# ACT's first weight load waits for GpSimd's identity matrix

## The chip, the cores and the metric

The kernel runs on one core of a Trainium2 chip. A core has five engines with queues of their own: TensorE (PE, matrix multiplies; PEld is its weight loads), VectorE (DVE), ScalarE (ACT), GpSimd (POOL) and SyncE (SP, which here only issues DMAs). They work at the same time and wait for each other by semaphores. DMAs are issued from SP and from ACT, each into a queue of its own, and are moved by 16 DMA engines that both queues share. The metric is the device time in microseconds of one execution; before the change it is 168.63 us, the median of 3 runs (168.02 to 168.94).

## The reference

Two branches work on the same input `x` (2048 positions of 512 values, bfloat16) and are mixed by a gate that each position computes for itself:

```python
x = A_x
g = _sigmoid((x * gate_w).sum(-1, keepdims=True))
a = _A_ref(x, A_wqkv, A_wo)
b = _B_ref(x, B_w1, B_b1, B_w2, B_b2)
return g * a + (1 - g) * b
```

Branch A is local attention: `x @ wqkv` gives queries, keys and values for 32 heads of 16 values. Each position attends to 8 positions, itself and those 2, 4, ... 14 before it; the result is multiplied by `wo`. Branch B is a layer norm over the 512 values of a position, followed by a two-layer network with a gelu that mixes over the 2048 positions (`w1` is 2048 x 1792, `w2` is 1792 x 2048).

## The kernel before, in words

Everything is kept in one SBUF arena and cut into tiles of 128 partitions. TensorE's work comes in four stages: the projections to queries, keys and values (line 619), the sums over a head's 16 values for the attention scores (line 698), the two layers of branch B (lines 812 and 862), and the output projection (line 878). VectorE does the attention's products and sums and the final mixing, ScalarE takes results out of PSUM and applies exp and gelu.

The kernel is first written down as a list of operations, each with its engine, its estimated duration, what it reads and writes and what it must wait for (`deps`: a wait on a semaphore; `order`: only a place in the order). A planner (`schedule`) then simulates the engines with these estimates and fixes the order on each engine; `plan_waits` leaves out the waits that are already implied. For the first loads the planner's landing times are given by hand (`lands`), and their `deps` are cleared, so that they are issued as early as their queue comes to them.

The projections need `x` transposed: 512 positions of a block along the free axis and the 512 values along partitions. Block 0 (the first 512 positions) is built from two sources:

- The first 128 values of each position are loaded as they stand, as "plain columns" (`d_xp`, line 479, SP's first DMA: 512 runs of 256 bytes, 128 KB). TensorE transposes them by multiplying with an identity matrix (`tr0`, `tr1`, line 545). ScalarE copies one half of the result out of PSUM (`ev_tra`, line 555) and VectorE the other (`ev_trb`, line 557).
- The other 384 values are transposed by the DMA itself (`d_xt0`, line 473, SP's second DMA).

The identity matrix is made by GpSimd (`ident`, line 417), its first operation after the constants. `tr0` waits for it, and VectorE's `rp` (line 424), which sums its columns into a small indicator matrix.

The query weights come in four loads of 128 rows each (`d_wp0_0` to `d_wp0_3`, 128 KB each, all with line 429). The first two are ACT's first two instructions, followed by the load of ACT's function table and `ev_tra`. The last two are issued by SP after `d_xt0`, and after them the key weights, `x` itself for the layer norm (`d_x0` and on), and the transposed reads of the later blocks (`d_xt1` and on, line 460).

TensorE begins with seven warm-up matmuls on constants (line 537), goes on with the four transposing matmuls, one more warm-up matmul, and then block 0's projections (`pf_...`, line 619): four that need `d_wp0_0` and the transposed plain columns, four that need `d_wp0_1` and `d_xt0`, four for `d_wp0_2`, four for `d_wp0_3`, then the keys' sixteen.

Of the kernel before, what the change touches and what calls it, by code (L numbers as in the profile page):

```python
# [333 lines left out]
def bass_gated_mix__sliding_local_dilated__mixer_token_mlp__prompt_kernel(nc, A_x, A_wqkv, A_wo, B_x, B_w1, B_b1, B_w2, B_b2, gate_w, out, dbg=None):  # L334
    with contextlib.ExitStack() as es:
# [75 lines left out]
        def psub(ap_, p0, np_, offs, dims):  # L411
# [5 lines left out]
        c_ident = A("pool", lambda e: e.affine_select(out=IDENT, in_=nc.const_aps.tensor(1.0, [128, 128], BF16), pattern=[[1, 128]], compare_op=ALU.is_equal,  # L417
                                                     fill=0.0, base=0, channel_multiplier=-1),
                    0.4, writes=["ident"], name="ident")
# [19 lines left out]
        def ld_x(t0, n, q="sp"):  # L439
            ds = sch.dsem("x%d" % t0)  # L440
            op = sch.dma(q, mk_dma(X[:, t0:t0 + n, :], xv[:, t0:t0 + n, :]), n * 128 * D * 2, ds,
                         writes=["x%d" % t for t in range(t0, t0 + n)], deps=throttle() if q == "sp" else [], after=prev_dma() if q == "sp" else [], name="d_x%d" % t0)
            if q == "sp":
                init_dmas.append(op)
            return op

        def ld_w(tn, d0, n, q="sp"):
            ds = sch.dsem("wqkv%d_%d" % (tn, d0))
            op = sch.dma(q, mk_dma(WQKV[:, d0:d0 + n, tn * D:(tn + 1) * D], wqkv_v[:, d0:d0 + n, tn * D:(tn + 1) * D]),
                         n * 128 * D * 2, ds, writes=["wqkv%d_%d" % (tn, dt) for dt in range(d0, d0 + n)],  # L450
                         deps=throttle() if q == "sp" and n == 4 else [], after=prev_dma() if q == "sp" else [],
                         issue=0.65 if n == 4 else 0.45, name="d_wp%d_%d" % (tn, d0))
            if q == "sp":
                init_dmas.append(op)
            return op
# [14 lines left out]
        def ld_xt0():  # L470
            ds = sch.dsem("xt0")
            dst = XT[:, 1:4, 0:512]
            op = sch.dma("sp", lambda e: e.dma_start_transpose(dst, x2d[0:512, 128:512]), 512 * 384 * 2, ds, issue=1.25,
                         writes=XT0[1:4], after=prev_dma(), name="d_xt0")
            init_dmas.append(op)
            return op
# [6 lines left out]
        first_loads = [ld_w(0, 0, 1, "act"), ld_xt0(), ld_w(0, 1, 1, "act"), ld_w(0, 2, 1), ld_w(0, 3, 1), ld_w(1, 0, 2), ld_w(1, 2, 2),  # L483
                       ld_x(0, 2)]
        ld_xt(1)
        first_loads.append(init_dmas[-1])
        for op_, t_ in zip(first_loads, (3.5, 5.7, 5.0, 6.3, 6.7, 7.6, 8.6, 9.4, 11.0)):
            op_.lands = t_
            op_.deps.clear()
        first_loads[2].order.add(first_loads[0])  # L490
        init_dmas[:] = [first_loads[1]] + first_loads[5:]
        ld_x(2, 2)
# [560 lines left out]
```

## Time and profile before

| | |
|---|---|
| median of 3 runs | 168.63 us (168.02 to 168.94) |
| the profiled execution | 168.55 us |
| its span, first to last instruction | 167.3 us |
| TensorE matmuls busy | 163.9 us (98%) |
| VectorE busy | 151.3 us (90%) |
| ScalarE busy | 75.0 us (45%) |
| GpSimd busy | 0.7 us |
| DMA | 29.64 MB, mean 177 GB/s |

The span is what the profile shows of one execution, from its first to its last instruction; some time lies around it. Busy time of TensorE is an upper bound, since matmuls are pipelined and overlap. The profile names groups of instructions by the line of the kernel, so that all plain DMAs, which one helper issues, have line 429, and are told apart by their tensors, engines and times. Times in the timeline are counted from the start of the span.

### The profile page before, as it was taken

How to read it: one execution, taken by the hardware profiler on the slowest of the kernel's cores; microseconds unless marked ns; L12 is line 12 of the kernel's file. 1: busy time of each engine (PE TensorE's matmuls, PEld its weight loads, DVE VectorE, ACT ScalarE, POOL GpSimd, SP SyncE). 2: the span in 40 equal slices, each digit the busy share in tenths (PEclk: the TensorE clock that was granted, in tenths of full speed). 3: DMA queues.
4: the chain of work that ended last, by engine and by line, in shares of the span. 5: the costliest groups of instructions: out<-in, count | busy, mean ns of one | idle time of the engine just before them, and what ended most of it. 6: DMA issues, size and time to landing. Idle time of an engine off the chain costs nothing.

```text
span 167.3 us, 2152 instructions
## 1 busy us (share of the span) xinstructions
PE 163.9 (98%) x860; PEld 77.6 (46%) x860; DVE 151.3 (90%) x154; ACT 75.0 (45%) x116; POOL 0.7 (0%) x8
## 2 busy tenths in 40 slices
PE   7999999999999999999999999999999999999994
PEld 2455555554454444444444444444444444444463
DVE  0145999999999999999999999999999999999896
ACT  3077688889899818793113121131231321310100
POOL 1000000000000000000000000000000000000000
DMA  5999999968003837996579936462672580000454
GB/s 130 315 272 262 303 322 291 307 196 246 0 0 97 311 115 187 303 290 153 133 183 343 335 129 143 112 187 68 184 218 83 138 223 0 0 0 0 157 190 159
DMA packets 47625, 29.64 MB, mean 177 GB/s; under 512 B 9856, under 2 KB 46464, under 8 KB 47616
## 3 DMA queue, kind: packets, MB, share of 16 engines
q1 hardware_dynamic: 45504, 24.85, 54.0%
q10 hardware_dynamic: 2112, 4.66, 10.0%
q8 instruction: 7, 0.11, 0.3%
q14 instruction: 2, 0.02, 0.0%
HBM read 21.24 MB, written 2.10 MB: 140 GB/s over the span
## 4 chain that ended last, share of the span: by engine, by line
PE 94%; DVE 3%; DMA 2%; issue 0%
PE ps L812 29%; PE ps L862 29%; PE ps L619 25%; PE ps L878 6%; PE ps L698 4%; DVE arena L899 2%; DMA arena<-in_A_x_dram 2%; PE ps L545 0%; DVE arena L557 0%
## 5 line engine op out<-in xcount | busy, mean ns | idle before, releaser
L812 PE MATMUL ps<-arena 128*128 128x512 bf16 x224 | 48.7, 379 | 0.0
L862 PE MATMUL ps<-arena 128*128 128x512 bf16 x224 | 48.7, 379 | 0.0
L619 PE MATMUL ps<-arena 128*128 128x512 bf16 x192 | 42.3, 382 | 0.1
L690 DVE TENSOR_TENSOR arena<-arena 128x4096 bf16<-128x4096 bf16 (+1 forms) x12 | 35.5, 2996 | 2.3 <-ACT arena L630 1.8
L797 DVE TENSOR_TENSOR arena<-arena 128x8192 bf16<-128x8192 bf16 x8 | 35.0, 4419 | 0.0
L812 PEld LDWEIGHTS ps<-arena 128*128 128x128 bf16 x224 | 21.8, 98 | 26.7 <-ACT arena L728 0.4
L862 PEld LDWEIGHTS ps<-arena 128*128 128x128 bf16 x224 | 21.9, 98 | 26.5
L619 PEld LDWEIGHTS ps<-arena 128*128 128x128 bf16 x192 | 21.6, 114 | 20.8 <-DVE arena L557 0.7
L930 ACT ACTIVATE arena<-ps,arena 128x512 bf16<-128x512 f32 x16 | 12.4, 778 | 39.4 <-PE ps L862 39.4
L800 DVE TENSOR_TENSOR arena<-arena 128x4096 bf16<-128x4096 bf16 (+1 forms) x16 | 27.0, 1752 | 0.0
L630 ACT ACTIVATE arena<-ps 128x512 bf16<-128x512 f32 x32 | 18.5, 596 | 4.5 <-PE ps L619 4.5
L833 ACT ACTIVATE arena<-ps,arena 128x512 bf16<-128x512 f32 x14 | 9.6, 687 | 22.2 <-PE ps L812 17.4
L574 DVE BATCH_NORM_STATS2 arena<-arena 128x6 f32<-128x512 bf16 x16 | 10.0, 680 | 5.6 <-DMA arena<-in_A_x_dram 5.6
L878 PE MATMUL ps<-arena 128*128 128x512 bf16 (+1 forms) x80 | 14.2, 337 | 0.0
L899 DVE SCALAR_TENSOR_TENSOR arena<-ps,arena 128x512 bf16<-128x512 f32 (+1 forms) x20 | 11.5, 638 | 0.9 <-PE ps L878 0.7
L598 ACT ACTIVATE arena<-arena 128x512 bf16<-128x512 bf16 x16 | 12.2, 806 | 0.0
L627 ACT ACTIVATE arena<-ps 128x512 bf16<-128x512 f32 x16 | 9.0, 596 | 5.5 <-PE ps L619 5.4
L878 PEld LDWEIGHTS ps<-arena 128*128 128x128 bf16 x80 | 7.8, 98 | 6.3
L674 DVE SCALAR_TENSOR_TENSOR arena<-arena 128x512 bf16<-128x512 bf16 x16 | 10.1, 685 | 0.0
L744 DVE TENSOR_TENSOR arena<-arena 128x512 bf16<-128x512 bf16 (+4 forms) x11 | 7.3, 667 | 0.6 <-ACT arena L763 0.2
L698 PE MATMUL ps<-arena 128*32 128x512 bf16 x128 | 7.3, 380 | 0.0
L728 ACT ACTIVATE arena<-ps 128x512 bf16<-128x512 f32 x8 | 4.7, 592 | 4.6 <-PE ps L698 4.6
(42 smaller groups left out, 40.5 us busy)
## 6 DMA issues: line engine op xcount, KB each, us to landing
arena<-in_B_w_dram SPq DMA_DIRECT2D x7, 1024.0 KB, 8.3
arena<-in_B_w_dram SPq DMA_DIRECT2D x8, 896.0 KB, 5.1
arena<-arena ACTq DMA_DIRECT2D x32, 128.0 KB, 3.0
arena<-in_A_x_dram SPq DMA_DIRECT2D x4, 512.0 KB, 5.1
out_dram<-arena SPq DMA_DIRECT2D x14, 128.0 KB, 1.7
arena<-in_A_x_dram SPq DMA_DIRECT2D x1, 1536.0 KB, 7.9
arena<-in_A_wqkv_dram SPq DMA_DIRECT2D x2, 256.0 KB, 3.6
arena<-in_A_x_dram SPq DMA_DIRECT2D x2, 256.0 KB, 3.5
```

The source lines that it names most:

```text
L598: A("act", (lambda t_: (lambda e: e.activation(out=X[:, t_, :], in_=X[:, t_, :], func=AF.Identity, scale=col(RSTD, t_), bias=col(NMR, t_)) ...
L619: ins = e.matmul(ps[:, bank, s0:s1], lhsT=lhsT, rhs=XT[:, dt, sb * 512 + s0:sb * 512 + s1], start=(dt == 0 and s0 == 0), stop=(dt == 3))
L630: return lambda e: e.activation(out=dst, in_=ps[:, bank, :], func=AF.Copy)
L690: return lambda e: e.tensor_tensor(out=PBL[buf][:, :, 512 * c0:512 * (c0 + nc_)], in0=in0, in1=in1, op=ALU.mult)
L698: ins = e.matmul(ps[32 * c:32 * c + 32, 4 + wl, :], lhsT=RP, rhs=PBL[buf][:, wl, c * 512:(c + 1) * 512], start=(dl == 0), stop=(dl == 3), ...
L797: A("dve", (lambda o_, i0, i1: (lambda e: e.tensor_tensor(out=o_, in0=i0, in1=i1, op=ALU.mult)))(pv, in0, in1), 4.4, reads=v_res + ["atx_% ...
L800: A("dve", (lambda pv_, n__: (lambda e: e.tensor_tensor(out=pv_[:, 0:n__], in0=pv_[:, 0:n__], in1=pv_[:, n__:2 * n__], op=ALU.add)))(pv, n ...
L812: ins = e.matmul(ps[:, bank, :], lhsT=W1W[:, slot, st, 128 * e_:128 * e_ + 128], rhs=X[:, st, :], start=(st == 0), stop=(st == NST - 1))
L862: ins = e.matmul(ps[:, bank, :], lhsT=W2S[slot][:, ft, 128 * e_:128 * e_ + 128], rhs=UT[:, ft, :], start=(ft == 0), stop=(ft == NFT - 1))
L878: ins = e.matmul(ps[:, bank, 0:c1 - c0], lhsT=OT[:, t, 128 * i:128 * i + 128], rhs=WO[:, t, c0:c1], start=(t == 0), stop=(t == 3))
L899: A("dve", (lambda i_, b_, c0_, c1_: (lambda e: e.scalar_tensor_tensor(out=T1[:, i_, c0_:c1_], in0=ps[:, b_, 0:c1_ - c0_], scalar=col(G, i ...
L930: A("act", (lambda i_, bank_: (lambda e: e.activation(out=T1[:, i_, :], in_=ps[:, bank_, :], func=AF.Identity, scale=col(OMG, i_), bias=co ...
```

## The change

Of the first loads, whose waits have just been cleared, the first (`d_wp0_0`, ACT's) is given one again: the operation that writes the identity matrix, on GpSimd. ACT then waits for that operation before it issues the load. ACT's instructions after it keep their order. The orders of the other engines stay as they were.

```diff
         for op_, t_ in zip(first_loads, (3.5, 5.7, 5.0, 6.3, 6.7, 7.6, 8.6, 9.4, 11.0)):
             op_.lands = t_
             op_.deps.clear()
+        first_loads[0].deps.add(c_ident)
         first_loads[2].order.add(first_loads[0])
         init_dmas[:] = [first_loads[1]] + first_loads[5:]
         ld_x(2, 2)
```

## The prediction

> **What bounds the kernel now.** I read the page first, for the busy shares, then the chain that ended last, then the timeline of the first microseconds, then the DMA's share and landings there.
>
> ```profile
> PE 163.9 (98%) x860; PEld 77.6 (46%) x860; DVE 151.3 (90%) x154; ACT 75.0 (45%) x116; POOL 0.7 (0%) x8
> ...
> PE   7999999999999999999999999999999999999994
> ```
>
> TensorE is full in every slice but the first and the last. So a change at the start can only move the moment from which TensorE runs without a gap, and the chain of waits says which moment that is (columns: start, length, what):
>
> ```profile
> 0.80 3.10 DMA arena<-in_A_x_dram
> 3.91 0.14 issue
> 4.04 0.60 PE ps L545 x4
> 4.64 0.02 issue
> 4.66 0.44 DVE arena L557
> 5.10 0.05 issue
> 5.15 33.44 PE ps L619 x152
> ```
>
> SP's first load, the plain columns (d_xp), lands at 3.91; four identity matmuls transpose it (tr0, tr1), VectorE copies the result out (ev_trb), and from 5.15 TensorE runs projections with no gap. From there the chain is TensorE's until 161.65 and then nearly 4 us of VectorE. Whatever d_xp gains or loses reaches 5.15 unchanged, unless something else the first projection waits for becomes the last: ACT's first weight load (d_wp0_0) or ACT's copy (ev_tra).
>
> The timeline shows what stands around the change (start, length, engine, line; a q marks an issue):
>
> ```profile
> 0.80 1.02 ACTq L429 DMA_DIRECT2D arena<-in_A_wqkv_dram  x2
> 0.80 0.43 SPq L429 DMA_DIRECT2D arena<-in_A_x_dram  x1
> 0.84 2.93 PE L537 MATMUL ps<-const-bfloat16-1.0 128*128 128x512 bf16 x7 [0.84 <-PEq L1038]
> 0.89 0.29 POOL L417 TENSOR_SCALAR_AFFINE_SELECT arena<-const-bfloat16-1.0 128x128 bf16<-128x128 bf16 x1 [0.38 <-POOLq L1038]
> ...
> 1.29 1.64 SPq L473 DMA_TRANSPOSE arena<-in_A_x_dram  x1
> ...
> 1.84 1.28 ACT L555 ACT_TABLE_LOAD   x1 [1.84 <-issue]
> ...
> 4.45 0.38 ACT L555 ACTIVATE arena<-ps 128x256 bf16<-128x256 f32 x1 [1.32 <-PE ps L545]
> ```
>
> And the DMA: first the issues with their time to landing (d_wp0_0, d_xp; then the transposed read d_xt0), then four stretches, whose last two columns are the share of the 16 DMA engines and GB/s:
>
> ```profile
> arena<-in_A_wqkv_dram ACTq DMA_DIRECT2D x1, 128.0 KB, 2.9
> arena<-in_A_x_dram SPq DMA_DIRECT2D x1, 128.0 KB, 3.1
> ...
> arena<-in_A_x_dram SPq DMA_TRANSPOSE x1, 4.4
> ```
>
> ```profile
> 1.80:2.20 0.40, 0.40 (x3) 0.13 (x1) 0.00 (x0) 0.36 (x1) 0.00 (x0) 1.00 0.16 40
> 2.20:2.60 0.40, 0.40 (x3) 0.12 (x2) 0.00 (x0) 0.40 (x1) 0.00 (x0) 1.00 0.61 116
> 2.60:3.00 0.40, 0.40 (x3) 0.12 (x2) 0.00 (x0) 0.40 (x1) 0.00 (x0) 1.00 1.01 312
> 3.00:3.40 0.40, 0.40 (x3) 0.07 (x1) 0.00 (x0) 0.13 (x1) 0.00 (x0) 1.00 1.20 329
> ```
>
> By the DMA view of the same stretches, SP's queue moved 62, 114, 108 and 239 packets and ACT's 0, 17, 99 and 84. The engines had room until 2.6; from 2.6 to 3.0 they were full and ACT's packets took 70.6% of them. Only there does d_wp0_0 visibly hold d_xp up.
>
> **The change part by part.** The sum goes by the profiled execution: 168.55 us, of which 167.30 is the span and 1.25 lies around it. That is 0.08 under the median, 168.63.
>
> *The wait on ACT.* The identity is written by 0.89 + 0.29 = 1.18, and VectorE's reduction that waits for it starts at 1.21. So ACT's first load is issued near 1.24 instead of 0.80: 0.44 later (0.41 to 0.49). Queued behind it on ACT, each 0.44 later: the second weight load (d_wp0_1, 1.26 to 1.70), the table load (ending at 3.12, then 3.56), and ev_tra. Their readers: d_wp0_0 lands at 0.80 + 2.9 = 3.7, then near 4.1, and is read at 5.15: 1 us of cover. d_wp0_1 landed 3.0 after its issue, at 4.3, then near 4.7; its reader is the fifth projection, at 6.48: 1.7 us. The table load is done 0.9 us before ev_tra's start at 4.45. Each costs nothing at these values. The price is open where ACT's loads now meet d_xt0, whose issue holds SP from 1.29 to 2.93; no row shows an ACT load issued wholly inside such a read. The nearest is d_wp0_1, issued at 1.26 with most of its 0.55 us inside it, and it landed in 3.0 us like the others: I take zero. The other end: it gets nothing out until that issue ends, and d_wp0_0 lands at 2.93 + 2.9 = 5.83. SP's queue is met too: if d_xt0's issue grows by what ACT's second load lost beside it (0.55 - 0.44 = 0.11) for each of two loads, SP's next one (d_wp0_2, issued at 2.99, landing 3.1 later at 6.1) comes 0.22 later, for the ninth projection at 7.34: covered. No order of instructions changes on any engine; ACT's first load has one more wait.
>
> *What d_xp gains.* At 2.6 it has moved 176 of its 512 packets, so 336 are left. If it goes on at 239 per 0.40 us (its pace from 3.0 on, with ACT still taking half), the 336 take 0.56 us and end near 3.16 instead of 3.4: 0.24 sooner. Lower end: nothing, since the pace of 62 and 114 packets while the engines had room says that it was also held back by something other than ACT. Upper end: tr0 can't start before the warm-up matmuls are through; their last, a half-width one, starts at 3.35 and its columns are in at 3.56, so 4.04 - 3.56 = 0.48. ACT's packets now begin near 2.64 and still share some of the stretch, so I take 0.2, near the lower row: d_xp lands at 3.7, the first projection starts at 4.95.
>
> *How much of it is kept: the clock.* The first projections are not at full speed:
>
> ```profile
> 5.56 0.63 PE L619 MATMUL ps<-arena 128*128 128x512 bf16 x1
> ...
> 5.98 0.45 PE L619 MATMUL ps<-arena 128*128 128x512 bf16 x1
> ...
> 6.26 0.38 PE L619 MATMUL ps<-arena 128*128 128x512 bf16 x1
> ```
>
> 5.15 to 5.56 to 5.98 is 0.41 to 0.42 each, as in the warm-up; 5.98 to 6.26 is 0.28; later ones are 48.7 / 224 = 0.217. So the speed doubles near 6.12 (the third had 0.28 = c + (0.43 - c)/2, c = 0.13). 0.97 us are run at half speed. If the doubling comes at that same time whatever TensorE does, starting 0.2 earlier means 0.2 more at half speed, worth 0.1: the gain is 0.10. If the doubling moves along with the start, it is 0.20. The granted-clock column reads 1.00 throughout and cannot tell. Seven unbroken warm-up matmuls (2.7 us) didn't bring it, which speaks for a time of its own; I take 0.10.
>
> The Trainium skill, "TensorE: Matmul & The Clock Gate", Part 1 (The HAM clock gate), speaks against the full gain: the activity window is free-running, it does not reset when a kernel starts, so the doubling is where the window ends. By that rule the sum is 168.45, without it 168.35; the spacing above agrees with a doubling, but one profile doesn't show what it hangs on.
>
> *What is late next.* The fifth projection needs d_xt0, landed at 1.29 + 4.4 = 5.7, for 6.48; with the earlier start it comes near 6.38. DMA engines that idle a little in 2.2 to 2.6 push d_xt0 back by at most the 17 packets of ACT's that ran there, 30.2% of 0.40 us, 0.12. It stays covered by about 0.5. VectorE's later gaps (0.41 at 42.2 and 0.72 at 157.4, both ended by TensorE) let the gain pass to the end. Sum: 0 + 0 - 0.20 + 0.10 = -0.10, so 168.45 for this execution, 168.53 from the median; I forecast 168.5.
>
> **The rivals.**
>
> *Nothing moves (the change does not do what it says).* d_xp's packets are paced by their own generation, ACT's only filled room. For it: the thin pace before 2.6. Against: the jump to 239 per 0.40 us just as d_wp0_0 ends. Time: 168.55 to 168.63.
>
> *Slower: ACT's load queues behind the transposed read.* Place: the first projection's wait for d_wp0_0; it decides once that lands after about 4.9, 1.2 later than now. At the bound of 5.83 TensorE starts at 5.85, 0.70 late. If the speed still doubles at 6.12, 0.27 instead of 0.97 us run at half speed, refunding 0.35: 168.55 + 0.35 = 168.9. If the pause makes TensorE earn the speed anew, at least the 2.7 us that did not suffice in the warm-up run at half: 0.70 + (2.7 - 0.97)/2 = 1.57, 170.1. For it: ACT's second load already took 0.55 to issue beside the read, where the first took 0.44. Against: it landed on time.
>
> *Faster: the pause closes.* d_xp lands by 3.43, warm-up and transposes run unbroken, and the double speed comes before the first projection: 0.48 sooner and 0.97/2 = 0.48 of slow time gone, 167.6. For it: 336 packets at the engines' full pace would be through near 3.0. Against: it needs both. The same section of the Trainium skill gives about 3.4 us of sustained work as what brings the clock; an unbroken run from 0.84 would reach that near 4.3. No run here shows such a start.
>
> **How the numbers follow.** Forecast, 168.3 to 168.55: 0.38. Nothing moves: 0.22. Slower: 0.24, of which 0.08 stays within 0.5% of the median and 0.16 is beyond. Faster: 0.16, of which 0.14 is beyond 0.5%. 0.5% is 0.84 us, 167.79 to 169.47, about what this kernel's measurement can tell (its three runs spread over 0.92). So faster 0.14, same 0.38 + 0.22 + 0.08 + 0.02 = 0.70, slower 0.16. The range runs from the fast case's 167.6 to 169.7, inside the slow case (168.9 to 170.1), and leaves out about 0.05 below and 0.13 above; the forecast's own is 168.3 to 168.6.
>
> **What would show it.** ACT's first issue near 1.24; d_xp landing near 3.7 and tr0 near 3.84; d_wp0_0 landing by 4.2; the first projection near 4.95 and released by VectorE, not by a weight load; the third or fourth projection again the one where the spacing halves, near 6.1 to 6.2. A first projection released by a DMA, or a doubling far from 6.1, would make the forecast wrong.

## The result and the profile after

The changed kernel takes 169.62 us (median of 15 runs, 168.83 to 171.62), the kernel before, run beside it, 168.48 us (15 runs, 167.94 to 169.98). The ratio is 1.0055, with a 95% interval of 1.0033 to 1.0077: slower, a little over half a per cent. The profile taken with these runs is of an unusually long execution (171.62 us, with a span of 170.4), so the lines below come from a second profile of the same kernel: 169.96 us, span 168.6, which is 1.3 us more than the 167.3 of before. In the runs taken with that second profile the changed kernel stood at 1.0083 (1.0059 to 1.0108).

From the changed kernel on, everything behind the added line has a line number one higher than before (L619 is L620), and the kernels of the experiments are shifted by up to three lines.

First the chain that ended last, changed kernel (start, length, what):

```profile
0.80 0.45 SPq L429
1.25 0.06 issue
1.31 6.42 DMA arena<-in_A_x_dram
7.73 0.04 issue
7.77 7.31 PE ps L620 x33
```

The chain no longer goes through the plain columns, the four identity matmuls and VectorE's copy. It goes through SP's second DMA, the transposed read d_xt0: issued at 1.31 as before, landed 6.42 later, at 7.73. Before it had taken 4.4. From 7.77 on TensorE runs without a gap.

The timeline of the changed kernel (start, length, engine, line; in brackets the idle time before and what ended it) shows that everything the change was about went as it should:

```profile
1.21 0.88 ACTq L429 DMA_DIRECT2D arena<-in_A_wqkv_dram  x2
1.31 1.88 SPq L473 DMA_TRANSPOSE arena<-in_A_x_dram  x1
...
3.56 0.63 PE L546 MATMUL ps<-arena 128*128 128x128 bf16 x4
...
4.71 1.59 PE L620 MATMUL ps<-arena 128*128 128x512 bf16 x4
...
7.77 6.45 PE L620 MATMUL ps<-arena 128*128 128x512 bf16 x29 [1.47 <-DMA arena<-in_A_x_dram]
```

ACT issues at 1.21, the transposing matmuls start at 3.56 instead of 4.04, the first projection at 4.71 instead of 5.15. Then four projections run and the fifth, the first that needs d_xt0 and ACT's second weight load (d_wp0_1), stands until 7.77. Before it ran at 6.48. 7.77 - 6.48 = 1.29 is the whole difference of the two spans (1.30): the 0.44 won at the first projection is lost in that wait, and 1.29 more.

The landings in the changed kernel, from the DMA issues (d_xp and d_wp0_0; then, from a later stretch, d_wp0_1 and d_xt0; the last column is us from issue to landing):

```profile
arena<-in_A_x_dram SPq DMA_DIRECT2D x1, 128.0 KB, 2.4
arena<-in_A_wqkv_dram ACTq DMA_DIRECT2D x1, 128.0 KB, 2.8
...
arena<-in_A_wqkv_dram ACTq DMA_DIRECT2D x1, 128.0 KB, 5.8
arena<-in_A_x_dram SPq DMA_TRANSPOSE x1, 6.4
```

d_xp takes 2.4 instead of 3.1. But d_wp0_1 takes 5.8 (1.63 to 7.47), and d_xt0 6.4 instead of 4.4. Both are late together. In before, d_wp0_1 took 3.0:

```profile
arena<-in_A_wqkv_dram ACTq DMA_DIRECT2D x1, 128.0 KB, 3.0
```

What the DMA engines did meanwhile, in stretches of before and then of the changed kernel (the last two columns are the engines' share and GB/s):

```profile
2.60:3.00 0.40, 0.40 (x3) 0.12 (x2) 0.00 (x0) 0.40 (x1) 0.00 (x0) 1.00 1.01 312
3.80:4.80 1.00, 0.76 (x5) 0.45 (x5) 0.14 (x1) 0.35 (x1) 0.00 (x0) 1.00 1.27 279
```

```profile
2.20:2.60 0.40, 0.40 (x3) 0.12 (x2) 0.00 (x0) 0.40 (x1) 0.00 (x0) 1.00 1.05 243
2.60:3.00 0.40, 0.40 (x3) 0.12 (x2) 0.00 (x0) 0.40 (x1) 0.00 (x0) 1.00 1.06 318
...
3.80:4.80 1.00, 0.91 (x6) 0.32 (x5) 0.42 (x1) 0.38 (x1) 0.00 (x0) 1.00 1.19 147
```

In 3.8 to 4.8 the engines are as busy as before (1.19 against 1.27) and move half as much: 147 GB/s against 279. That second is d_xt0's. The DMA view of it by queue, of before and then of the changed kernel (q1 is SP's queue, q10 ACT's; packets, MB, share of the 16 engines):

```profile
q1 hardware_dynamic: 1090, 0.28, 127.4%
```

```profile
q1 hardware_dynamic: 380, 0.10, 89.5%
q10 hardware_dynamic: 56, 0.05, 29.7%
```

Before, ACT's queue was empty in it, both its loads being through by 3.8. In the changed kernel d_xp is through sooner, so d_xt0's first packet comes at 2.91 instead of 3.51. ACT's second load is issued later, and its first packet comes at 3.11, about where it came before (3.17). So its packets no longer run ahead of d_xt0's but among them, and the last comes at 6.76 instead of 3.75.

### The profile page after: what moved, and what is told of

The parts are those of the page before. It is cut to its first block, busy times and chain, and to the rows that moved or that the text cites. A ratio compares the mean times of both kernels' runs of the same rounds, so it can differ in the third digit from the quotient of the medians.

```text
span 170.4 us, 2152 instructions
## 1 busy us (share of the span) xinstructions
PE 165.2 (97%) x860; PEld 78.1 (46%) x860; DVE 151.3 (89%) x154; ACT 75.1 (44%) x116; POOL 0.7 (0%) x8
## 4 chain that ended last, share of the span: by engine, by line
PE 92%; DMA 4%; DVE 2%; SPq 0%; issue 0%
PE ps L813 28%; PE ps L863 28%; PE ps L620 25%; PE ps L879 6%; PE ps L699 4%; DMA arena<-in_A_x_dram 4%; DVE arena L900 2%; SPq L429 0%
## 5 line engine op out<-in xcount | busy, mean ns | idle before, releaser
L620 PE MATMUL ps<-arena 128*128 128x512 bf16 x192 | 43.7, 390 | 2.1 <-DMA arena<-in_A_x_dram 2.1
L620 PEld LDWEIGHTS ps<-arena 128*128 128x128 bf16 x192 | 21.8, 115 | 24.1 <-DMA arena<-in_A_x_dram 2.5
L675 DVE SCALAR_TENSOR_TENSOR arena<-arena 128x512 bf16<-128x512 bf16 x16 | 10.1, 687 | 0.0
```

The lines of the kernel that those rows point to most:

```text
L620: ins = e.matmul(ps[:, bank, s0:s1], lhsT=lhsT, rhs=XT[:, dt, sb * 512 + s0:sb * 512 + s1], start=(dt == 0 and s0 == 0), stop=(dt == 3))
```

## The experiments

One table first. Landings and the fifth projection's start are those of one profiled execution of each kernel, in us from the start of its span; the ratio is against the kernel before on the same chip, with its 95% interval.

| kernel | d_xp | d_wp0_1 | d_xt0 | fifth projection | ratio |
|---|---|---|---|---|---|
| before | 3.91 | 4.31 | 5.73 | 6.48 | |
| the change, again | 3.21 | 7.47 | 7.73 | 7.77 | 1.0083 (1.0059 to 1.0108) |
| change, second load on SP | 3.19 | 6.04 | 5.52 | 6.38 | 1.0044 (1.0027 to 1.0061) |
| before, second load later | 3.85 | 7.31 | 7.54 | 7.58 | 1.0110 (1.0080 to 1.0139) |
| before, second load on SP | 3.87 | 6.07 | 5.37 | 6.21 | 1.0045 (1.0028 to 1.0061) |
| before, third load nobody reads | 3.88 | 4.38 | 7.55 | 7.60 | 1.0081 (1.0061 to 1.0100) |
| same, 32 KB | 3.88 | 4.33 | 6.21 | 6.26 | 1.0021 (1.0007 to 1.0035) |
| same, 128 KB in 256-byte packets | 3.88 | 4.32 | 6.95 | 7.00 | 1.0056 (1.0044 to 1.0069) |
| change, ACT's loads merged | 3.11 | 4.56 | 6.03 | 6.39 | 0.9998 (0.9985 to 1.0010) |
| before, ACT's loads merged | 4.27 | 4.60 | 5.84 | 7.20 | 1.0099 (1.0063 to 1.0135) |
| same, longer warm-up | 4.41 | 4.71 | 5.92 | 6.34 | 1.0013 (0.9999 to 1.0028) |
| change, SP's loads paired | 3.15 | 7.12 | 5.43 | 7.26 | 1.0047 (1.0031 to 1.0063) |
| before, longer warm-up | 3.88 | 4.30 | 5.74 | 6.83 | 1.0007 (0.9992 to 1.0022) |

Where the fifth projection starts more than 0.2 behind both landings, it waited for no load but followed the fourth. Its start then hangs on when the first one started and on when TensorE's speed doubled in that one execution.

**The change once more.** The kernel is the changed one.

> The changed kernel once more, for a profile beside the disturbed-looking one. Theory M (mixing): ACT's second weight load (d_wp0_1), issued near 1.64, shares the DMA engines with the packets of the transposed read d_xt0, both go slower, and the fifth projection waits for them: d_xt0 lands at 6.2 to 7.8 instead of 5.73, wait 0.4 to 2.1 us, time 169.2 to 169.9. Theory Q (issue): ACT's issues beside SP's transposed issue hold SP: that issue takes 1.9 to 2.0 instead of 1.64, and d_xt0 lands later by just those 0.3 (near 6.0). Theory K (clock): the loads land as before within 0.2 and the doubling of the matmul speed merely falls later than 6.1, near 7 to 9.

Measured: d_xt0 at 7.73, wait 1.47, time 169.95. SP's issue of d_xt0 took 1.88, 0.24 more than before, while d_xt0 was 2.00 later, so Q alone can't be it. The speed doubled near 5.9, so K isn't either: d_xt0 was not where K wanted it. It fits M, which was formed on the first profile of this kernel.

**Only the second load later.** No identity for the first load; the second waits for VectorE's `rp`.

```diff
-        A("dve", f_rp, 0.2, reads=["ident"], writes=["rp"], name="rp")
+        rp_ = A("dve", f_rp, 0.2, reads=["ident"], writes=["rp"], name="rp")
...
+        first_loads[2].deps.add(rp_)
         first_loads[2].order.add(first_loads[0])
```

> The kernel before, with only ACT's second weight load made later: it waits for VectorE's indicator reduction (rp, done at 1.50), so it is issued near 1.54 instead of 1.26; the first load stays at 0.80. M: d_xp lands at 3.9 as before, but d_wp0_1 runs further into d_xt0's packets: d_xt0 lands at 6.0 to 7.5, the fifth projection waits 0.2 to 1.5, time 168.7 to 169.7. Q: SP's transposed issue takes 1.64 to 1.8, d_xt0 lands within 0.2 of 5.73, time 168.3 to 168.7. K: no change, 168.5.

Its chain and its TensorE timeline at the fifth projection:

```profile
1.30 6.23 DMA arena<-in_A_x_dram
7.54 0.05 issue
7.58 7.31 PE ps L620 x33
```

The second load was issued at 1.53 instead of 1.26, 0.27 us later, and d_xt0 landed 1.81 later, with d_xp where it was (3.85). So a landing of d_xp as early as in the changed kernel isn't needed for the loss; the second load's lateness is enough. By packets, the second load and d_xt0 begin together here, at 3.24; in before the load was 0.34 ahead.

**A third load that nobody reads.** This takes the weight load itself out of the question. 128 KB more on ACT's queue, of a destination that is free then:

```diff
+        XD = view("OUTS", BF16, [(1, 512)], extra=512)
+        d_ex = sch.dma("act", mk_dma(XD, wqkv_v[:, 1, 0:512]), 128 * 512 * 2, sch.dsem("extra"), writes=["outs1"], after=[first_loads[2]], issue=0.45, name="d_extra")
+        d_ex.lands = 6.0
         init_dmas[:] = [first_loads[1]] + first_loads[5:]
```

> The kernel before with a third load on ACT, of 128 KB that nobody reads (a copy of the second's data into SBUF that is free then), issued after the second, near 1.8, so that its packets meet those of d_xt0. Both weight loads stay where they were. Theory M (packets of ACT's queue among those of the transposed read slow the read): d_wp0_1 lands by 4.4 as before, d_xt0 lands at 6.5 to 7.7 instead of 5.73, and the fifth projection waits for d_xt0 alone, 0.3 to 1.5 us; time 168.7 to 169.8. Theory L (in the changed kernel only the late weight load itself counts, d_xt0's lateness comes from elsewhere, as from SP's longer issue): d_xt0 lands at 5.7 to 6.0, time within 0.3 of before.

Its DMA issues (d_wp0_1, d_xt0) and TensorE's timeline:

```profile
arena<-in_A_wqkv_dram ACTq DMA_DIRECT2D x1, 128.0 KB, 3.1
arena<-in_A_x_dram SPq DMA_TRANSPOSE x1, 6.2
```

```profile
5.12 1.05 PE L622 MATMUL ps<-arena 128*128 128x512 bf16 x4 [0.21 <-DVE arena L560]
7.60 6.67 PE L622 MATMUL ps<-arena 128*128 128x512 bf16 x30 [1.43 <-DMA arena<-in_A_x_dram]
```

Both weight loads landed as before, and yet d_xt0 was 1.82 late and TensorE waited for it alone. Theory L falls: a load on ACT's queue whose packets run among those of the transposed read makes the read late, whoever needs the load.

**How much, and in what packets.** The third load again, with 32 KB in 128 packets of 256 bytes, and with 128 KB in 512 packets of 256 bytes (these are columns of `x` instead of `wqkv`):

```diff
-        XD = view("OUTS", BF16, [(1, 512)], extra=512)
-        d_ex = sch.dma("act", mk_dma(XD, wqkv_v[:, 1, 0:512]), 128 * 512 * 2, ...
+        XD = view("OUTS", BF16, [(1, 128)], extra=512)
+        d_ex = sch.dma("act", mk_dma(XD, wqkv_v[:, 1, 0:128]), 128 * 128 * 2, ...
```

```diff
-        XD = view("OUTS", BF16, [(1, 512)], extra=512)
-        d_ex = sch.dma("act", mk_dma(XD, wqkv_v[:, 1, 0:512]), 128 * 512 * 2, ...
+        XD = view("OUTS", BF16, [(128, 4), (1, 128)], extra=512)
+        d_ex = sch.dma("act", mk_dma(XD, xv[:, 4:8, 0:128]), 512 * 128 * 2, ...
```

> As the kernel with the third load that nobody reads, but that load is 128 packets of 256 bytes (32 KB) instead of 128 of 1 KB. M by the number of packets (each turn between the queues costs): d_xt0 as late as with the large one, 6.5 to 7.7. M by bytes: a quarter of that lateness, d_xt0 at 5.9 to 6.3. Theory L: 5.7.

> As the kernel with the third load of 128 KB that nobody reads, but in 512 packets of 256 bytes instead of 128 of 1 KB. Theory B (bytes): what ACT's queue moves beside d_xt0 counts, so d_xt0 lands as late as there, 7.2 to 7.8, time 169.4 to 170. Theory S (size of the packet): only long packets between the short ones of the transposed read make it slow; d_xt0 lands at 6.2 to 6.7, time 168.4 to 169.

d_xt0's landing, in the order 32 KB, 128 KB in short packets:

```profile
arena<-in_A_x_dram SPq DMA_TRANSPOSE x1, 4.9
```

```profile
arena<-in_A_x_dram SPq DMA_TRANSPOSE x1, 5.6
```

The stretch from 3.8 to 4.8 with 128 KB in long packets, then in short ones:

```profile
3.80:4.80 1.00, 0.78 (x5) 0.46 (x5) 0.16 (x1) 0.37 (x1) 0.00 (x0) 1.00 1.23 187
```

```profile
3.80:4.80 1.00, 0.79 (x5) 0.46 (x5) 0.16 (x1) 0.38 (x1) 0.00 (x0) 1.00 1.26 265
```

A quarter of the bytes in as many packets costs d_xt0 0.48 us, about a quarter of 1.82, so it isn't the number of packets. The same bytes in short packets cost 1.22, between the two expectations: neither B nor S is right alone. The long packets are the worse ones: the engines move 187 GB/s beside them and 265 beside the short ones (from 4.4 to 5.4, where both loads are fully under way, 154 and 261). At before's 279 GB/s 128 KB by themselves would be 0.47 us, an estimate; the rest, 0.75 with short packets and 1.35 with long ones, is what the mixture costs.

All three of these loads were issued at the same time (1.74 or 1.75, for 0.45 or 0.46 us), while SP was issuing d_xt0. So the place of the issue by itself accounts for at most the 0.48 of the smallest one. No run has the packets run together for long without such an issue.

**Nothing beside the transposed read.** The second weight load on SP, behind d_xt0, with and without the change:

```diff
-        first_loads = [ld_w(0, 0, 1, "act"), ld_xt0(), ld_w(0, 1, 1, "act"), ld_w(0, 2, 1), ...
+        first_loads = [ld_w(0, 0, 1, "act"), ld_xt0(), ld_w(0, 1, 1), ld_w(0, 2, 1), ...
```

> The change, and ACT's second weight load moved to SP, behind d_xt0: nothing of ACT's runs beside d_xt0 but the end of d_wp0_0. M: d_xp lands near 3.1 as in the changed kernel, d_xt0 lands by 5.8, d_wp0_1 near 6.1, the first projection starts near 4.7; the fifth waits at most 0.5 us; time 168.0 to 168.7, below the changed kernel by 0.9 or more. Q: ACT's one issue still meets d_xt0's, SP's issue takes 1.8, d_xt0 lands near 5.9; time 168.5 to 169. K: 169.3 to 169.8, as the changed kernel.

> The kernel before without the wait, ACT's second weight load moved to SP behind d_xt0. M: d_xp lands at 3.6 to 3.9 (only d_wp0_0 beside it), d_xt0 at 5.3 to 5.7, d_wp0_1 near 6.1; time 168.1 to 168.6. Q: SP's issue takes 1.5 and all its later loads come 0.1 sooner, time 168.4. K: 168.5.

d_xt0 landed at 5.52 and 5.37, sooner than before, with SP's issue of it at 1.80 and 2.05 us, longer than before's 1.64. That ends Q: a longer issue goes with an earlier landing. But the times were missed: both kernels are slower than before, by 0.44 and 0.45%, though in their profiles the fifth projection started 0.10 and 0.27 sooner. SP has one load more to issue, and what follows is later. Without the change the 0.27 were lost again by the seventeenth projection: it waited for the first key weights, issued at 4.97 instead of 4.08 and landed at 9.03, and started at 9.07 as in before. (The rest of that kernel's loss is open: its profile is of the fastest of its six executions and has before's span.) In the changed kernel with this edit, d_xt1 was issued at 6.22 instead of 5.58 and took 6.5:

```profile
arena<-in_A_x_dram SPq DMA_TRANSPOSE x1, 6.5
```

```profile
4.71 7.87 PE L620 MATMUL ps<-arena 128*128 128x512 bf16 x32
12.90 3.40 PE L620 MATMUL ps<-arena 128*128 128x512 bf16 x14 [0.31 <-ACT arena L631]
```

TensorE stopped before 12.90. The view names ACT, but ACT's copies ended at 12.41 and 12.91, the later one after this matmul had started. d_xt1's landing, 6.22 + 6.5, lies 0.14 before it, and TensorE's wait for that load ended at 12.84. The matmul came 0.69 after its predecessor instead of 0.22: 0.47 lost.

**SP's list made short again.** The same kernel with the third and fourth query loads made one (the lines are set against the changed kernel, so that both edits show):

```diff
-        first_loads = [ld_w(0, 0, 1, "act"), ld_xt0(), ld_w(0, 1, 1, "act"), ld_w(0, 2, 1), ld_w(0, 3, 1), ...
+        w00, xt0, w01, w02 = ld_w(0, 0, 1, "act"), ld_xt0(), ld_w(0, 1, 1), ld_w(0, 2, 2)
+        first_loads = [w00, xt0, w01, w02, w02, ...
```

> The change, ACT's second weight load on SP behind d_xt0, and the third and fourth query loads made one of 256 KB, so that SP issues as many loads as before. Theory M: d_xp near 3.1, d_xt0 near 5.5, d_wp0_1 near 6.05; the wait of 0.47 us that the kernel with the second load on SP had for d_xt1 at 12.9 goes, since d_xt1 is issued near 5.75 instead of 6.22; time 168.0 to 168.5, 0.4 below that kernel. If the loss there was not SP's longer list, 168.9.

The stop at 12.9 went (d_xt1 landed at 11.85), and the time did not come down, because d_wp0_1 now landed at 7.12:

```profile
3.34 3.78 DMA arena<-in_A_wqkv_dram
7.12 0.14 issue
7.26 7.29 PE ps L621 x33
```

It took 3.78 from its issue, against 2.9 in the kernel without the pairing, where it is the same DMA at the same place of the queue. Why is open. What the pair shows is that this way of keeping the queues apart gains nothing.

**ACT's loads made one.** One load of 256 KB, after the identity and without waiting for it:

```diff
-        first_loads = [ld_w(0, 0, 1, "act"), ld_xt0(), ld_w(0, 1, 1, "act"), ld_w(0, 2, 1), ...
+        w01 = ld_w(0, 0, 2, "act")
+        first_loads = [w01, ld_xt0(), w01, ld_w(0, 2, 1), ...
...
-        first_loads[2].order.add(first_loads[0])
```

> The change, with ACT's two weight loads made one of 256 KB, issued near 1.21 after the identity. Its packets come without the second issue's 0.42 us between. M: d_xp lands near 3.2, the weights by 4.5, d_xt0 meets only their tail and lands at 5.5 to 6.3; the fifth projection waits less than 0.6; time 168.0 to 168.8. Theory L: as the changed kernel, 169.4 to 170.

> The kernel before, ACT's two weight loads made one of 256 KB, issued at 0.80. M: weights through by 3.6, before d_xt0's packets begin; d_xp lands at 3.9 to 4.2, d_xt0 near 5.7; time 168.1 to 168.6, as before. Theory L: the same.

With the change (and its wait kept), the landings of the merged load and of d_xt0 are:

```profile
arena<-in_A_wqkv_dram ACTq DMA_DIRECT2D x1, 256.0 KB, 3.4
arena<-in_A_x_dram SPq DMA_TRANSPOSE x1, 4.7
```

ACT's packets were through by 3.6 and d_xt0's had hardly begun. d_xt0 landed at 6.03 instead of 7.73, and the loss is gone: 0.9998 instead of 1.0083. This is the change with its wait kept and the meeting taken away, and it ends where before stood: d_xp's 0.8 are won (3.11) and the first projection starts at 4.71, but in this profile the fifth starts at 6.39, only 0.09 sooner than in before. It waited for no load, since d_xt0 had landed at 6.03: the four projections before it ran at half speed, 0.42 apart.

Without the wait the merged kernel lost 1%, against both theories, and no projection waits for a load in its profile. Its weight loads (PEld, which come one per matmul) show why:

```profile
4.38 0.34 PEld L545 LDWEIGHTS ps<-arena 128*128 128x128 bf16 x4 [1.31 <-issue]
...
9.34 0.15 PEld L619 LDWEIGHTS ps<-arena 128*128 128x128 bf16 x1 [0.28 <-issue]
9.76 0.15 PEld L619 LDWEIGHTS ps<-arena 128*128 128x128 bf16 x1 [0.28 <-issue]
10.17 1.84 PEld L619 LDWEIGHTS ps<-arena 128*128 128x128 bf16 x9 [0.26 <-issue]
```

The matmuls are 0.43 apart until 10.1; in the kernel before the speed doubled at 6.1. d_xp landed at 4.27, so TensorE stood from 3.56 to 4.41, between its warm-up and the transposes. To test whether that pause is the cause, the warm-up was made longer, in this kernel by two matmuls and in the kernel before by one:

```diff
-        A("pe", f_warm(6), 2.56, writes=["lg7_0", "lg7_1"], name="warm1", prio=-100)
+        A("pe", f_warm(8), 2.56, writes=["lg7_0", "lg7_1"], name="warm1", prio=-100)
```

> The kernel before with ACT's two loads made one (which lost 1% though no projection waited for a load), with eight full warm-up matmuls instead of six, so that TensorE is busy until 4.4, when d_xp has landed. Theory C (the longer pause of 3.56 to 4.41 cost TensorE a window of its clock): the speed doubles by 6.5 instead of 10.1 and the time falls to 168.3 to 168.9. Theory D (the loads themselves cost it): 169.8 to 170.2 as there.

> The kernel before with seven full warm-up matmuls instead of six, which fills its pause of 3.56 to 4.04. Theory C: as before or a little faster, 167.9 to 168.4, since fewer executions find the speed doubled late. Theory D: 168.3.

With eight, the merged kernel is at 1.0013 instead of 1.0099, and its projections run at full speed from their start (32 weight loads in 6.62 us, 0.21 each):

```profile
5.45 6.62 PEld L619 LDWEIGHTS ps<-arena 128*128 128x128 bf16 x32 [0.64 <-DVE arena L557]
```

All twelve of its executions took less than 169.2 us; of the six without the longer warm-up, five took more than 169.7. So the pause was the cause there. In the kernel before, whose pause is 0.48, filling it made no difference (1.0007).

## Why the prediction was wrong

It forecast 168.5, a gain of 0.1; the time went up by 0.93 (0.55% of 168.48). That it just stayed in the range is luck: the range's upper part came from a rival with a wait at another place. By its own steps:

- *The wait on ACT.* Right: first issue at 1.21 (forecast 1.24), d_wp0_0 landed at 3.98 (4.1), in time for the first projection; the table load was done at 3.40, 0.6 before ACT's copy at 4.02.
- *What d_xp gains.* Too small: 0.70 instead of 0.2, which brought the full 0.48 of the upper end to the transposes and 0.44 to the first projection. The thin pace of d_xp before 2.6 was read as held back by something other than ACT, since the engines had room. From 2.2 to 2.6 SP's queue moved 340 packets after the change, 114 before, and the engines' share was 1.05 instead of 0.61. Room on the engines wasn't room for d_xp. How ACT's load holds it back there, with 17 packets of its own, is open.
- *d_wp0_1 beside d_xt0: "I take zero".* This is the step that failed. The nearest row was d_wp0_1 of before, issued at 1.26, just ahead of d_xt0's issue, and landing in 3.0. That row is near in the time of issue, but its packets hardly met d_xt0's: ACT's last ones were gone by 3.8, d_xt0's first ones came at 3.5. The change brings d_xt0's forward to 2.91 and leaves the load's at 3.11, so that they run together; d_wp0_1 then took 5.8 and d_xt0 6.4, and the fifth projection waited 1.47. The row used was one in which the disputed thing hardly happened.
- *What is late next.* d_xt0 was named as next in line, with 0.12 as the most that it could be pushed back. That counted the engines' time for the displaced packets at an unchanged price. It was pushed back by 2.00, because the price of every packet rose: 147 GB/s at a share of 1.19.
- *The clock.* The speed doubled near 5.9 in the second profile of the changed kernel (the fourth projection followed the third by 0.37), near the 6.1 of before although the start was 0.44 sooner. It made no difference: the first four projections, at whatever speed, were done before the wait ended. The question of half or whole gain never arose, because of the wait. But the moment of the doubling, 6.1, belongs to that one execution of before, and not to the kernel: of the two profiles of the changed kernel, the first shows full speed from its first projection on (4.72) and the second only from 5.9. So the 0.97 us at half speed, and with them the half of the gain that the sum takes off, rest on one execution. No run tells how much of an earlier start is kept: with the meeting taken away the ratio is 0.9998 (0.9985 to 1.0010), which holds the forecast 0.10 as well as nothing.
- *The rivals.* The slower one had the right two transfers, ACT's load and the transposed read, and the wrong reader: it priced d_wp0_0 at the first projection, where the wait came at the fifth, for d_wp0_1 and d_xt0. It also took the cause to be the order of issue; two kernels with a longer issue and an earlier d_xt0 showed that it is not.

## What to carry to other kernels

A wait that lets one transfer run alone moves others, and the question is whom they now run beside, packet by packet, and not only when they are issued. A transposing DMA on one queue is worth keeping clear of plain loads on the other: here 128 KB beside it cost 1.2 to 1.8 us, where their bytes alone would be 0.47. It is worth it only if the load's new place costs nothing else, as the two kernels with one load more on SP's queue showed. To cost a meeting that the trace doesn't show, take a row in which the two really overlap, or keep the whole range open.

## What the runs showed of the hardware

- Two plain loads on ACT's and SP's queues moved 312 GB/s together at a share of 1.01 (before, 2.6 to 3.0), with no loss of throughput to be seen: SP's plain load almost alone moved 243 at 1.05 (changed kernel, 2.2 to 2.6). A plain load among the packets of a transposed read costs both: 147 GB/s at 1.19 in the changed kernel, against 279 at 1.27 for the read alone. The Trainium skill, "DMA: Bandwidth & Descriptors", section "Issuing engines are not separate DMA queues", says that DMAs issued by different engines run on the same 16 DMA engines and interleave. The traces agree, and show a price for it in this pairing. Why the packets take longer is not shown.
- When TensorE's speed doubles differs from execution to execution (from 4.72 or sooner and from 5.9 in the two profiles of the changed kernel). With a pause of at most 0.48 us behind the warm-up, seven profiles show full speed from the first projection on (which started between 4.71 and 5.45), and six a doubling between 5.8 and 6.9. With a pause of 0.85 (3.56 to 4.41) it came at 10.1, and filling that pause took the loss away (1.0013 instead of 1.0099). The Trainium skill, "TensorE: Matmul & The Clock Gate", Part 1 (The HAM clock gate), gives a free-running window of about 3.4 us in which activity is watched. The first profile of the changed kernel agrees with that length: after a wait of 2.06 us the granted clock was 0.50 from 7.9 to 11.3. How much work a window needs no run here shows.
